# Two rows of x to a partition, and a convolution on quarters of TensorE's array

## The chip, the cores and the metric

The kernel runs on one core of a Trainium2 chip. The time is device microseconds (us) of that core. Before the change the median of three runs is 176.09 us (176.07 to 176.24). TensorE (PE in the profile) multiplies into PSUM; VectorE (DVE) and ScalarE (ACT) copy PSUM out; GpSimd (POOL) issues the loads, SyncE (SP) most stores.

## What is computed

```
x   : 8 x 3264 x 192      weight : 8 heads x 7 taps      w_r, w_i : 64 x 192 x 192     w_ch : 192 x 192
w   = softmax(weight)
c   [b, s, h] = sum over k of w[h, k] * x[b, s - 6 + k, h]        causal, zeros ahead of row 0; 24 channels a head
C   = rfft(c over s), first 64 modes;   Y = C times (w_r + i w_i), mode by mode
y   = irfft(Y, 3264 rows);              u = c + y
out = u + relu(u @ w_ch)
```

Everything is multiplied in bf16 and summed in fp32; the result is fp32.

## The kernel before, in words

**Load.** x is cut into four pairs of sequences (q = 0 to 3). Each sequence is cut in halves of 1632 rows, and a half into 6 blocks (b) of 256 rows and a rest of 96 rows. The loads are issued by GpSimd, which also casts fp32 to bf16 on the way. `load_unit` (L169) loads 128 rows of the four half sequences of a pair at a time: partition p holds row p, so each packet is one row of 192 values, 384 B in bf16. `load_rest` (L179) loads the rests in 4 DMAs of 112 partitions. All of x stays in SBUF in `xall`. Behind x in the same queue come `moe_w_ch` and then the mode weights W (`load_w`, L299): 16 groups g of two DMAs each. Groups 0 to 7 go into `ct` of q = 2 and 3, groups 8 to 11 into a ring of four buffers in `arena`, groups 12 to 15 into the same ring again once the product of the group four before has been made (L501).

**First stage.** `units` (L53 to 55) lists the pieces in order, from q = 0 up and within a q from the last block down: for q = 0 five small ones, then three per q with two blocks each, the last one with the rest. For each unit (loop at L454) `conv_pass` (L312) runs four times, for two heads at a time. The convolution is a product with a banded matrix `bd3` of 128 rows: a main product and one for the six rows from the tile before. Each takes all 128 rows of the array and one half (64) of its columns; its outputs come in two row parities (`a`), so that afterwards partition p holds rows 2p and 2p + 1. The result is copied from PSUM (three pairs of banks, `cz`, in rotation) back into `xall`, three passes by ScalarE (L346), one by VectorE (L344). `fold` (L348, VectorE) makes the sum and the difference of the two halves of each sequence in `cpm`; `dft` (L354) multiplies them with the cosine and sine table `ftab` into the 64 modes (even modes need sums, odd ones differences, so sums and differences go to the two column halves). After the last unit of a q, `xtrans` (L372) turns its modes into the layout of the W products (`xt`). `c_bank` (L420) transposes the convolved rows into `ct`, eight transposes to a PSUM bank and then one copy (L393 to 398, VectorE three times in five, else ScalarE); `g_bank` (L400) does the same for the table of the inverse transform. These 42 transpose banks (`tjobs`, L435) are a list from which the code takes some wherever TensorE is to have work: one per unit from the seventh unit on (L465), ten between the last unit and the first W product (L474 to 488).

**Second part of the load.** The loop at L827 runs over the 16 groups of W. `mix(g)` (L493) is the product with group g, which waits for its W. Beside it run transpose banks in the number that the tuple in L827 gives, `mix_copy` and `mix_trans` for odd g, from g = 8 to 12 the products of five pairs of second-stage items ahead of time (`c_beside`, L662, in two phases), and a filler (`keep_busy`, L815). Banks and `c_beside` share four PSUM banks (`lt`).

**Second stage.** After g = 15, for each of 104 items (128 partitions, one row parity, two sequences) five products per row half of the array make c @ w_ch plus the inverse transform (`product`, L635), ScalarE clamps (L690), VectorE adds and SyncE stores (L712, L732). A planner written in the kernel (`second_stage`, L743) sets their order. The two row halves of the array take turns on a PSUM bank by a `nop` that waits for the other half's last product (L639).

The order on each engine is the order of the program (`manual_schedule`, L150).

Of the kernel before, what the change touches and what calls it, by code (L numbers as in the profile page):

```python
# [19 lines left out]
def kernel(  # L20
# [19 lines left out]
    P = 128  # L40
# [8 lines left out]
    PW = 32 + KK - 1  # L49
# [3 lines left out]
    UNITS0 = ((5, 1, 0), (4, 1, 0), (3, 1, 0), (1, 2, 0), (0, 1, 1))  # L53
    UNITS = ((4, 2, 0), (2, 2, 0), (0, 2, 1))
    units = [(q,) + u for q in range(NQ) for u in (UNITS if q else UNITS0)]

# [12 lines left out]
    xall = sb("xall", [NQ, 2, TQ, D], BF16)  # L69
    band = sb("band", [max(H * 2 * P, MODES // 8 * 2 * D)], BF16)  # L70
# [8 lines left out]
    wb = sb("wb", [D], BF16)  # L79
    ident = sb("ident", [P], BF16)  # L80
    ascale = sb("ascale", [1], F32)
    halfpi = sb("halfpi", [1], F32)
    sgn = sb("sgn", [1], F32)
    NK = 5
# [7 lines left out]
    yall = band[:, :].rearrange("p (n g d) -> p n g d", g=2, d=D)  # L92
    dram = ctx.enter_context(tc.tile_pool(name="dram", bufs=1, space=bass.MemoryType.DRAM))
    yrows = dram.tile([2, MODES // 2, 2 * B, D], BF16, tag="yrows", name="yrows")
    bd3 = band[:, 0:H * 2 * P].rearrange("p (h c) -> p h c", h=H)
# [18 lines left out]
    xdone = xall[:, 0, :, :, :].rearrange("p t k d -> p (t k d)")  # L114
# [18 lines left out]
    packed = temp(G4 * PW, BF16)  # L133
# [9 lines left out]
    masks = temp(KK * PW, U16)  # L143
# [3 lines left out]
    cpm = arena[:, NWA * WGB - FB:NWA * WGB].rearrange("p (r a k d) -> p r a k d", r=2, a=2, k=4)  # L147
    assert pos[0] <= NWA * WGB - FB
# [20 lines left out]
    def load_unit(q, b0, nb, rest):  # L169
        for t in range(2 * b0, 2 * b0 + 2 * nb):  # L170
            k = 2 + 4 * (t // 2)
            src = bass.AP(tensor=x.tensor, offset=x.offset + (2 * q * S + P * t) * D,
                          ap=[[D, P], [HS * D, 4], [1, D]])
            nc.gpsimd.dma_start(out=xall[:, q, t % 2, k:k + 4, :], in_=src)  # L174


    R0 = P - RR - 16

    def load_rest():  # L179
        for i in range(2):  # L180
            for t in range(2):
                off = (i * S + HS * (2 - t) - (P - R0)) * D
                src = bass.AP(tensor=x.tensor, offset=x.offset + off,
                              ap=[[D, P - R0], [2 * S * D, NQ], [1, D]])
                nc.gpsimd.dma_start(out=xall[R0:P, :, t, i, :], in_=src)

# [4 lines left out]
    load_unit(*units[0])  # L191
# [5 lines left out]
    for u in units[1:4]:  # L197
        load_unit(*u)
    load_rest()
    nc.vector.memset(packed, 0.0)  # L200
    nc.scalar.copy(out=bd3[:, :, PW:2 * P], in_=packed[:, 0:1].unsqueeze(2).to_broadcast([P, H, 2 * P - PW]))
# [6 lines left out]
    for k in range(KK):  # L208
        nc.vector.tensor_scalar(out=masks[:, PW * k:PW * (k + 1)], in0=cidx, scalar1=qoff[:, 0:1],
                                scalar2=float(KK - 1 - k), op0=ALU.add, op1=ALU.is_equal)  # L210
# [20 lines left out]
    pk3 = packed.rearrange("p (h c) -> p h c", h=G4)  # L231
    for k in range(KK):
        nc.vector.copy_predicated(out=pk3,
                                  mask=masks[:, PW * k:PW * (k + 1)].unsqueeze(1).to_broadcast([P, G4, PW]),
                                  data=ta3[:, :, k:k + 1].to_broadcast([P, G4, PW]))
    for g in range(4):
        for r in range(4):
            dst = bd3[32 * r:32 * r + 32, G4 * g:G4 * (g + 1), 32 * r:32 * r + PW]
            srcv = pk3[32 * g:32 * g + 32, :, :]
# [9 lines left out]
    def table(step):  # L249
# [10 lines left out]
        else:  # L260
            nc.vector.memset(xall[0:R0, :, :, 0:2, :].rearrange("p q t i d -> p (q t) (i d)"), 0.0)
# [3 lines left out]

    for u in units[4:6]:
        load_unit(*u)
# [4 lines left out]

    nc.gpsimd.memset(ident[:], 0.0)
    select(ident[:], 1.0, 0, [[-1, P]])

    nc.gpsimd.memset(order, 0.0)
    nc.gpsimd.memset(perm, 0.0)
    for c in range(2):
        cols = slice(MODES * c, MODES * (c + 1))
        ov = order[:, cols].rearrange("p (j r) -> p j r", r=2)  # L280
        pv = perm[:, cols].rearrange("p (j r) -> p j r", r=2)
        select(ov, 1.0, -JH * c, [[-1, JH], [-2 * JH, 2]])
        select(pv, 1.0 if c else -1.0, -JH * (1 - c), [[-1, JH], [-2 * JH, 2]])
    for u in units[6:8]:
        load_unit(*u)
    for u in units[8:]:
        load_unit(*u)
# [24 lines left out]
    def conv_pass(q, b0, nb, rest, h2):  # L312
        z = next_pair()
        nk = 4 * nb + 2 * rest
        k0 = 2 + 4 * b0 - 2 * rest

        def put(j, a, half, main, k, n, t, ks, step=1):
            h = 2 * h2 + j
            c0 = a + (0 if main else P)
            o = z[64 * half:64 * half + 64, j, GRP * nk * a:GRP * nk * (a + 1)].rearrange(  # L320
                "p (k e) -> p k e", e=GRP)[:, k - k0:k - k0 + step * (n - 1) + 1:step, :]
            nc.tensor.matmul(o, bd3[:, h, c0:c0 + P - 1:2],  # L322
                             xall[:, q, t, ks:ks + n, GRP * h:GRP * h + GRP],
                             start=(main and a == 0), stop=not main, tile_position=(0, 64 * half),
                             skip_group_check=True)

        for j in range(2):
            for a in range(2):
                for half in range(2):
                    put(j, a, half, True, k0, nk, half, k0)  # L330
# [562 lines left out]
```

## Time and profile before

| | |
|---|---|
| median of three runs | 176.09 us |
| the profiled execution | 175.52 us |
| its span on the core | 173.7 us |
| busy: PE, DVE, ACT, POOL | 149.5, 125.6, 118.8, 66.0 us |
| last DFT of the last unit but one ends the convolution's stretch (L366) | 68.81 us |
| first product with W (L498) | 77.70 us |
| product g = 14 | 105.10 us |

The span is the time from the first instruction to the last on the core; the profiled execution's time holds 1.8 us more, around it. In the lists, L is a line of the kernel, and an arrow in brackets names what ended the idle time before an instruction. A matmul's duration is modelled and matmuls overlap, so the pace is read from the starts of two rows and the count between them.

### The profile page before, as it was taken

To read this page: it belongs to the slowest core of one execution; us is meant where nothing else is said; L and a number is where in the kernel's file an instruction comes from. 1 tells how busy PE (TensorE), PEld (TensorE's weight loads), DVE (VectorE), ACT (ScalarE), POOL (GpSimd) and SP (SyncE) were. 2 spreads that over 40 slices of the span, in tenths; PEclk is the share of its full clock that TensorE was granted. 3 is DMA by queue.
4 is the path that set the end of the run, shared out by engine and by line. 5 is a ranking of instruction groups with operands and counts; after the bars stand their busy time and mean duration, and the time that the engine had idled before them with its cause. 6 is when DMAs were issued, how large, how long until landed. Compare 5 with 4: busy or idle time off the path is not lost.

```text
span 173.7 us, 6647 instructions
## 1 busy us (share of the span) xinstructions
PE 149.5 (86%) x2837; PEld 127.8 (74%) x2837; DVE 125.6 (72%) x246; ACT 118.8 (68%) x224; POOL 66.0 (38%) x108
## 2 busy tenths in 40 slices
PE   0044898899999999799998899999999999999980
PEld 0043797789889889577865565788999988999950
DVE  3892868476778778675545542499998999999990
ACT  6369356658686686755874654588889899898850
POOL 7977997775775584344234300420000000000000
PEclk9999999999999999999999999999999999999995
DMA  2999999999999999999999996359969999999996
GB/s 17 166 173 189 193 188 191 191 189 192 191 190 191 192 204 206 206 206 206 207 208 206 207 205 115 88 191 389 388 233 396 351 357 383 337 339 385 386 356 196
DMA packets 51650, 40.85 MB, mean 235 GB/s; under 512 B 30020, under 2 KB 51524, under 8 KB 51620
## 3 DMA queue, kind: packets, MB, share of 16 engines
q0 software_dynamic: 36400, 20.06, 83.2%
q1 hardware_dynamic: 14948, 20.16, 32.5%
q8 instruction: 22, 0.36, 0.8%
q10 hardware_dynamic: 272, 0.20, 0.3%
q14 instruction: 8, 0.07, 0.1%
HBM read 39.62 MB, written 20.45 MB: 346 GB/s over the span
## 4 chain that ended last, share of the span: by engine, by line
DMA 46%; PE 37%; POOL 9%; issue 3%; DVE 1%; POOLq 0%; DVEq 0%
DMA xall<-in_x_dram 23%; PE outleft L644 18%; DMA arena<-in_moe_w_i_dram 13%; DMA ct<-in_moe_w_i_dram 11%; PE sumright L644 8%; PE mixright L644 8%; POOL xall L174 7%; DVE xall L712 1%; PE sumright L498 1%; PE trleft L429 1%; POOL loose L270 1%; PE sumright L818 0%; PE mixright L526 0%; PE mixright L548 0%; POOL arena L303 0%
## 5 line engine op out<-in xcount | busy, mean ns | idle before, releaser
L322 PEld LDWEIGHTS <-band 128*64 128x64 bf16 x944 | 38.7, 121 | 18.3 <-ACT band L241 11.1
L644 PEld LDWEIGHTS <-ct 64*128 64x128 bf16 x624 | 41.0, 94 | 4.8 <-PE trleft L644 0.5
L322 PE MATMUL cvleft<-xall,band 128*64 128x192 bf16 (+4 forms) x640 | 30.5, 248 | 13.9 <-ACT band L241 11.1
L644 PE MATMUL outleft<-mixa,gtab 64*128 64x384 bf16 x182 | 41.9, 323 | 0.1
L174 POOL DMA_DIRECT2D xall<-in_x_dram x48 | 36.0, 760 | 10.2 <-DMA xall<-in_x_dram 8.4
L644 PEld LDWEIGHTS <-gtab 64*128 64x128 bf16 x416 | 30.9, 94 | 3.0 <-PE outleft L644 1.1
L644 PE MATMUL outleft<-wa,ct 64*128 64x192 bf16 x208 | 30.4, 243 | 0.0
L351 DVE TENSOR_TENSOR arena<-xall 128x1536 bf16<-128x1536 bf16 (+1 forms) x28 | 22.4, 840 | 8.2 <-ACT xall L346 7.8
L690 ACT ACTIVATE outleft<-outleft 128x384 f32<-128x384 f32 x53 | 24.4, 477 | 4.6 <-PE outleft L644 2.3
L346 ACT CAST xall<-cvleft 128x768 bf16<-128x768 f32 (+3 forms) x29 | 21.4, 756 | 8.8 <-PE cvleft L322 7.3
L644 PE MATMUL sumright<-mixa,gtab 64*128 64x384 bf16 x92 | 25.8, 323 | 0.0
L644 PE MATMUL mixright<-mixa,gtab 64*128 64x384 bf16 x90 | 25.8, 323 | 0.0
L644 PE MATMUL outleft<-wb,ct 64*128 64x192 bf16 x104 | 23.3, 243 | 0.0
L398 DVE COPY ct<-trleft 128x1024 bf16<-128x1024 bf16 (+1 forms) x19 | 12.4, 662 | 12.7 <-PE trleft L429 7.8
L322 PE MATMUL cvright<-xall,band 128*64 128x192 bf16 (+4 forms) x304 | 15.9, 247 | 1.6 <-DVE xall L344 1.2
L396 ACT COPY ct<-trleft 128x1024 bf16<-128x1024 bf16 x13 | 13.2, 1012 | 4.6 <-PE trleft L426 2.4
L712 DVE TENSOR_TENSOR arena<-outleft,xall 128x384 f32<-128x384 f32 x27 | 14.4, 553 | 2.5 <-PE outleft L644 2.1
L346 ACT CAST xall<-cvright 128x768 bf16<-128x768 f32 (+3 forms) x13 | 9.8, 751 | 8.4 <-PE cvright L322 6.1
L644 PE MATMUL sumright<-wa,ct 64*128 64x192 bf16 x88 | 14.2, 243 | 0.0
L644 PE MATMUL mixright<-wa,ct 64*128 64x192 bf16 x80 | 13.8, 243 | 0.0
L426 PEld LDWEIGHTS <-xall 128*128 128x128 bf16 x208 | 11.7, 98 | 2.6 <-issue 0.3
L690 ACT ACTIVATE sumright<-sumright 128x384 f32<-128x384 f32 x26 | 12.3, 477 | 1.4 <-PE sumright L644 0.3
(147 smaller groups left out, 283.2 us busy)
## 6 DMA issues: line engine op xcount, KB each, us to landing
xall<-in_x_dram POOLq DMA_DIRECT2D x48, 192.0 KB, 7.9
out_dram<-arena SPq DMA_DIRECT2D x23, 384.0 KB, 4.0
out_dram<-xall SPq DMA_DIRECT2D x13, 384.0 KB, 4.1
out_dram<-ct SPq DMA_DIRECT2D x8, 384.0 KB, 4.6
ct<-in_moe_w_r_dram POOLq DMA_DIRECT2D x8, 288.0 KB, 9.4
ct<-in_moe_w_i_dram POOLq DMA_DIRECT2D x8, 288.0 KB, 10.4
arena<-in_moe_w_r_dram POOLq DMA_DIRECT2D x8, 288.0 KB, 10.5
arena<-in_moe_w_i_dram POOLq DMA_DIRECT2D x8, 288.0 KB, 10.9
```

Source lines behind the costliest of these rows:

```text
L174: nc.gpsimd.dma_start(out=xall[:, q, t % 2, k:k + 4, :], in_=src)
L270: nc.gpsimd.affine_select(out=dst, in_=dst, compare_op=ALU.not_equal, fill=fill, base=base, pattern=pattern, channel_multiplier=1)
L322: nc.tensor.matmul(o, bd3[:, h, c0:c0 + P - 1:2], xall[:, q, t, ks:ks + n, GRP * h:GRP * h + GRP], start=(main and a == 0), stop=not main, ...
L346: nc.scalar.copy(out=dst, in_=srcv)
L351: nc.vector.tensor_tensor(out=cpm[:, r, :, 0:2 * nb, :], in0=src[:, :, :, 0, :], in1=src[:, :, :, 1, :], op=op)
L396: nc.scalar.copy(out=out, in_=in_)
L398: nc.vector.tensor_copy(out=out, in_=in_)
L426: nc.tensor.transpose(o, cv[:, blk, 0:P], ident[:])
L429: nc.tensor.transpose(o[64 * i:64 * i + 64, :], cv[:, i, P:D], ident[:], tile_position=(0, 64 * i))
L644: m = nc.tensor.matmul((Z[s % NZ] if bank is None else bank)[:, cols], l, r, start=start, stop=stop, skip_group_check=True)
L690: act = nc.scalar.activation(out=z, in_=z, func=ACT.Relu)
L712: add = nc.vector.tensor_tensor(out=o[:, :, a, :], in0=Z[s % NZ][:, 0:2 * D].rearrange("p (i d) -> p i d", i=2), in1=c_rows(q, kk)[:, a, : ...
```

## The change

1. **x comes two rows to a partition.** Partition p of a block gets rows 2p and 2p + 1 in one packet of 768 B (in bf16); a DMA loads 128 partitions of one half and two sequences, still 192 KB, two to a block. The rest takes 4 DMAs of 48 partitions. The 16 partitions ahead of a rest, once zeros, get the last 32 rows of the block before, moved by a product (`rows_ahead`), and copied by both ScalarE and VectorE.
2. **The convolution runs on quarters.** Input parity b to output parity a, 64 rows to 64 columns: four products per (a, b), one on each quarter of the array, the two of the upper row half (`src` 0) at once, the two of the lower row half three steps later (`LAG`). Each output parity has a PSUM bank of its own, and the lower row half starts on a bank only when the upper one has left it (a `nop` with a wait, twice per head). The band holds 258 columns a head in place of 256, and is made from 144 columns in place of 76, with four masks in place of seven.
3. **Six large units**, from q = 3 down to q = 0, that may span two q: 4, 4, 4, 5, 3 and 4 blocks, one head at a time. Six heads are copied by ScalarE and heads 3 and 6 by VectorE (half and half in the first unit). The previous unit's folds are issued after heads 1, 3 and 5, into three buffers that now fill the whole arena; its DFT comes after the last head. No transposes run in the convolution any more.
4. **The last unit has no folds**: its DFT multiplies both halves with `ftab` and with `fneg` (the same, odd modes negated) on the full array, 18 products.
5. **Transposes**: a row of `ct` is cut in three full 128 x 128 blocks in place of two full and two half ones; the second stage gets a third copy of weights (`wc`) for it. Twelve banks stand between the last unit and the first W product, and the tuple beside the W products becomes (1, 2, 2, 2, 2, 2, 2, 3, 3, 3, 3, 3, 2, 2, 0, 0).

```diff
-    UNITS0 = ((5, 1, 0), (4, 1, 0), (3, 1, 0), (1, 2, 0), (0, 1, 1))
-    UNITS = ((4, 2, 0), (2, 2, 0), (0, 2, 1))
+    units = [[(3, 4, 2, 0), (3, 2, 2, 0)], [(3, 0, 2, 1), (2, 4, 2, 0)], [(2, 2, 2, 0), (2, 0, 2, 1)],
+             [(1, 4, 2, 0), (1, 2, 2, 0), (1, 1, 1, 0)], [(1, 0, 1, 1), (0, 4, 2, 0)], [(0, 2, 2, 0), (0, 0, 2, 1)]]
...
+            q, b = blocks.pop(0)
+            for h in range(2):
+                k = 2 + 4 * b + 2 * h
+                src = bass.AP(tensor=x.tensor, offset=x.offset + (2 * q * S + HS * h + 2 * P * b) * D,
+                              ap=[[2 * D, P], [S * D, 2], [1, 2 * D]])
+                nc.gpsimd.dma_start(out=xall[:, q, k:k + 2, :, :].rearrange("p k t d -> p k (t d)"), in_=src)
...
+    def rows_ahead(q):
+        k = 2 + 4 * (NBH - 1)
+        z = next_pair()
+        for i in range(2):
+            for h in range(2):
+                nc.tensor.matmul(z[64 * (1 - h):64 * (1 - h) + 64, i, 0:2 * D], ahead[64:P, :],
+                                 xall[64:P, q, k + 2 * h + i, :, :].rearrange("p t d -> p (t d)"), start=True,
+                                 stop=True, tile_position=(64, 64 * (1 - h)), skip_group_check=True)
+        for h, engine in enumerate((nc.scalar.copy, nc.vector.tensor_copy)):
+            r = slice(64 * (1 - h), 64 * (1 - h) + R0)
+            engine(out=xall[r, q, 0:2, :, :].rearrange("p i t d -> p i (t d)"), in_=z[r, :, 0:2 * D])
...
+    def conv_head(u, h, engine):
+        z = next_pair()
+        f0, f1 = extent(u)
...
+        def put(src, dst, c, a, b, fa, fb, back=0, start=False, stop=False):
+            r = slice(64 * src, 64 * src + 64)
+            base = c + (0 if a == b else PB - 1 + a)
+            return nc.tensor.matmul(z[64 * dst:64 * dst + 64, a, GRP * (fa - f0):GRP * (fb - f0)],
+                                    bd3[r, h, base:base + 64], xflat[r, fa - back:fb - back, b, cols], start=start,
+                                    stop=stop, tile_position=(64 * src, 64 * dst), skip_group_check=True)
+
+        def later(a, b, name):
+            if a == b:
+                nop = nc.tensor.nop()
+                tc.add_manual_dep(nop.ins, name[-1], mybir.DependencyInfo(
+                    mybir.DependencyClass.Sync, mybir.DependencyReason.DATA), reason="row tiles take turns on a bank")
+            put(1, 1, 0, a, b, f0, f1, stop=a != b)
+            for k, (fa, fb) in enumerate(spans):
+                put(1, 0, 64, a, b, fa, fb, 4, stop=a != b and k == len(spans) - 1)
+            if a == 1 and b == 0:
...
+                if engine == "v":
+                    nc.vector.tensor_copy(out=dst, in_=srcv)
+                else:
+                    nc.scalar.copy(out=dst, in_=srcv)
+
+        for a in range(2):
+            last = []
+            for b in (a, 1 - a):
+                put(0, 1, 64, a, b, f0, f1, start=a == b)
+                last.append(put(0, 0, 0, a, b, f0, f1, start=a == b).ins.name)
+                upper.append(lambda a=a, b=b, name=last: later(a, b, name))
+                flush(LAG)
...
+            if cpm is None:
+                ops.append((ftab[:, t, :], call[:, q, 1 + 2 * b, a, :, :], slice(0, P)))
+                ops.append((fneg[:, t, :], call[:, q, 2 + 2 * b, a, :, :], slice(0, P)))
...
     for k, u in enumerate(units):
...
+        for q, b0, nb, rest in u:
+            if b0 + nb == NBH:
+                rows_ahead(q)
+        todo = []
+        for h in range(H):
+            conv_head(u, h, "v" if h in ((1, 3, 5, 7) if k == 0 else (3, 6)) else "a")
+            if k == 0 and h in (1, 3, 5):
+                table(h // 2)
+            if prev and h in (1, 3, 5):
+                piece = prev.pop(0)
+                todo.append((*piece, fold(*piece)))
+        flush()
+        for q in pend:
+            xtrans(q)
+        pend = [d[0] for d in todo if d[3]]
+        for d in todo:
+            dft(*d)
+        prev = list(u)
+    lt += hand_out("left", "tr", (1, 1, 1, 1))
     for g in range(NWC + NWA):
         load_w(g)
-    trans_banks(3)
+    trans_banks(2)
     rot[0] = 2
-    xtrans(NQ - 1)
+    for q in pend:
+        xtrans(q)
+    for piece in prev:
+        dft(*piece, None)
+    trans_banks(8)
+    rot[0] = 2
+    xtrans(0)
     ye = hand_out("right", "mix", (1, 1))
     trans_banks(2)
...
-    for g, beside in enumerate((0, 1, 1, 2, 2, 2, 1, 2, 2, 2, 2, 2, 2, 2, 0, 0)):
+    for g, beside in enumerate((1, 2, 2, 2, 2, 2, 2, 3, 3, 3, 3, 3, 2, 2, 0, 0)):
```

More of the change, by code (lines that the diff above doesn't have):

```diff
@@ L142 @@
     qoff = temp(1, F32)
-    masks = temp(KK * PW, U16)
+    NE4 = (KK + 1) // 2
+    masks = temp(NE4 * PW, U16)
     sidx = temp(NTF, F32)
@@ L817, in keep_busy @@
         for _ in range(n):
-            nc.tensor.matmul(sums[bank][:, 0:2 * D], ident[:], xall[:, 0, 0, 0:2, :], start=True, stop=True,
+            nc.tensor.matmul(sums[bank][:, 0:2 * D], ident[:], call[:, 0, 0, 0, :, :], start=True, stop=True,
                              skip_group_check=True)
@@ L825, in beside_pair @@
             tb[0] += 2 * phase
-    for g, beside in enumerate((0, 1, 1, 2, 2, 2, 1, 2, 2, 2, 2, 2, 2, 2, 0, 0)):
+    for i in range(2):
+        nc.scalar.copy(out=wc[64 * i:64 * i + 64, :], in_=wa[64 * (1 - i):64 * (1 - i) + 64, :])
+    for g, beside in enumerate((1, 2, 2, 2, 2, 2, 2, 3, 3, 3, 3, 3, 2, 2, 0, 0)):
         d = g // 2
```

224 lines of the change are left out of this document (100 added, 124 removed).

## The prediction

> **What bounds the kernel now.** I read the page from the top: the busy shares, then the slices, then the chain.
>
> ```profile
> PE 149.5 (86%) x2837; PEld 127.8 (74%) x2837; DVE 125.6 (72%) x246; ACT 118.8 (68%) x224; POOL 66.0 (38%) x108
> DMA  2999999999999999999999996359969999999996
> GB/s 17 166 173 189 193 188 191 191 189 192 191 190 191 192 204 206 206 206 206 207 208 206 207 205 115 88 191 389 388 233 396 351 357 383 337 339 385 386 356 196
> DMA 46%; PE 37%; POOL 9%; issue 3%; DVE 1%; POOLq 0%; DVEq 0%
> ```
>
> Two halves show. For 24 slices (104 us) the DMA engines are full with loads: x, then the mode weights W at a higher rate. After a dip the results go out, and the chain of waits is TensorE's. So the chain names DMA for the load half. But a full DMA engine only says that there is always something to move; whether TensorE keeps up must be read from its own timeline.
>
> ```profile
> 59.22 0.85 PE L322 MATMUL cvleft<-xall,band 128*64 128x192 bf16 x16
> 59.90 0.82 PE L366 MATMUL sumright<-arena,ftab 128*64 128x384 bf16 x8
> 60.55 0.49 PE L366 MATMUL sumright<-xall,ftab 128*64 128x384 bf16 x4
> ...
> 62.20 0.22 PE L378 MATMUL cvleft<-loose 128*64 128x128 bf16 x1
> ...
> 62.59 0.85 PE L322 MATMUL cvright<-xall,band 128*64 128x192 bf16 x16
> ...
> 68.81 0.86 PE L366 MATMUL sumright<-arena,ftab 128*64 128x384 bf16 x8
> ...
> 77.70 0.71 PE L498 MATMUL sumright<-ct,mixa 128*16 128x192 bf16 x24 [0.17 <-ACT mixa L389]
> ...
> 87.73 0.46 PE L498 MATMUL sumright<-arena,mixa 128*16 128x192 bf16 x12
> ...
> 93.64 0.46 PE L498 MATMUL sumright<-arena,mixa 128*16 128x192 bf16 x12 [0.72 <-DMA arena<-in_moe_w_i_dram]
> ...
> 96.51 0.46 PE L498 MATMUL sumright<-arena,mixa 128*16 128x192 bf16 x12 [0.43 <-DMA arena<-in_moe_w_i_dram]
> 96.90 1.07 PE L426 MATMUL trleft<-ident,xall 128*128 128x128 bf16 x16
> 97.90 0.34 PE L644 MATMUL trleft<-wa,ct 64*128 64x192 bf16 x4
> 98.07 0.25 PE L644 MATMUL trleft<-wb,ct 64*128 64x192 bf16 x2
> 98.25 0.40 PE L526 MATMUL mixright<-ident,band 128*128 128x128 bf16 x4
> 98.48 0.33 PE L818 MATMUL sumright<-xall,ident 128*128 128x384 bf16 x1
> 98.74 0.34 PE L644 MATMUL trleft<-wa,ct 64*128 64x192 bf16 x4
> ...
> 105.10 0.46 PE L498 MATMUL sumright<-arena,mixa 128*16 128x192 bf16 x12
> ```
>
> The convolution ends at 68.8, the products with W start at 77.70 (groups g = 0 and 1), g = 8 is at 87.73, g = 10 at 93.64, g = 14 at 105.10. Only from g = 10 on does TensorE wait for W, and only 0.72, 0.43 us and less per group of 2.87 us. **TensorE is thus nearly as late as the DMA.** A faster load alone gains little unless TensorE's own path to g = 14 gets shorter; that path is what I add up. From g = 14 on nothing in the order of work changes, so the end moves as g = 14 moves.
>
> **What TensorE's pieces cost (same rows).** Sixteen convolution products of 192 columns take 59.22 to 59.90: 42 ns each, where two column halves run side by side. At 2.4 columns per ns (the 16 transposes of 128 columns, 96.90 to 97.90, say about the same) 192 columns in two halves would be 40 ns. A DFT pair takes 0.163 us (eight products, 59.90 to 60.55). xtrans is 0.4 us (62.20 to 62.59). A transpose bank (8 transposes) is 0.50 us. In the W loop a group costs 0.40 for mix, 0.35 for each phase of c_beside, 0.23 for mix_trans (every other group), 0.27 for keep_busy. Test on the old loop: from g = 0 to g = 8 it has 8 mixes, 11 banks and 4 mix_trans, 3.2 + 5.5 + 0.9 = 9.6; the rows say 10.03, so I add 4%.
>
> **The load (part 1 of the change).**
>
> ```profile
> 0.00:10.00 10.00, 0.00 (x0) 0.00 (x0) 6.43 (x31) 4.63 (x5) 8.86 (x18) 1.00 0.93 100
> 10.00:57.00 47.00, 40.91 (x883) 36.99 (x885) 32.81 (x55) 31.09 (x50) 34.91 (x54) 1.00 1.59 190
> 62.00:102.00 40.00, 37.24 (x757) 28.82 (x751) 24.22 (x41) 26.13 (x40) 16.67 (x28) 1.00 1.21 206
> ...
> xall<-in_x_dram POOLq DMA_DIRECT2D x48, 192.0 KB, 7.9
> xall<-in_x_dram POOLq DMA_DIRECT2D x4, 168.0 KB, 7.8
> 35.05 1.18 PE L322 MATMUL cvleft<-xall,band 128*64 128x192 bf16 x24 [0.66 <-DMA xall<-in_x_dram]
> ```
>
> The first three rows are stages of the windows view and end in granted clock, DMA share and GB/s; two are DMA issues, the last is TensorE's timeline. x moves at 190 in packets of 384 B (192 bf16), W at 206 in packets of 1152 B. Per engine (a sixteenth) that is 32.3 and 89.5 ns a packet; a straight line through both gives 3.7 ns plus 74.5 ns per 1000 B, so the new 768 B packets take 60.9 ns: 202 GB/s. The bounds are 190 (no gain) and 206; I take 202 as the line between the two rows. x shrinks from 48 x 192 KB + 4 x 168 KB = 10.13 MB to 10.03 (the rest has 48 partitions of 768 B in place of 112 of 384). With 1.0 MB moved by 10 us, x ends at 58.05 before and 54.7 after: **3.35 us earlier**, and W with it. POOL still issues 48 + 4 DMAs, half the packets each, in the same gaps between its memsets and selects; it is 38% busy and waits on landings, so I cost it at nothing.
>
> The Trainium skill (DMA: Bandwidth & Descriptors, section Specifications) says that below 512 B a transfer falls short of line rate, as the engine must read before it writes. By that rule the new packets run at W's 206, which takes 0.6 us off the sum below; the rows show the slower 384 B, none shows 768 B.
>
> When is data usable? At 35.05 TensorE gets the 24th x DMA, 5.41 MB with the rest, while 5.76 had moved: landing lags by 1.8 us. Each unit needs its own blocks (0.393 MB each), the rest from the second on, and the block below. So unit 1 (9 blocks) can start at 27.3, unit 3 (18) at 44.8, unit 4 (21) at 50.7, unit 5 (all) at 56.5.
>
> **The convolution (part 2).** A unit is 8 heads of 4 steps; a step is 4 products on the four quarters of the array, N = 24 x (16, 18, 18, 20, 14, 18) columns, and 3 steps of lag are half empty at the unit's end: 35 steps. If four quarters run side by side a step takes N/2.4, but not below 4 x 42 = 168 ns. That gives 6.3, 6.3, 7.0, 5.9, 6.3 us for units 1 to 5. No row shows quarters. Bounds: four at a time as above, or only two, twice the time. I take four, since the row at 59.22 shows column halves side by side and the second stage row halves (the stage row's PE column holds the count):
>
> ```profile
> 115.00:167.00 52.00, 52.00 (x893) 48.28 (x891) 49.04 (x97) 45.69 (x105) 0.00 (x0) 1.00 0.98 355
> ```
>
> 893 products of on average 269 columns (three of 192, two of 384) in 52 us are 58 ns each; one alone would need 112. The two waits per head before the lower rows take a bank stand behind two more steps of the upper rows (0.34 us), so I cost them at nothing; uncovered they cost up to 0.1 us each, 1.6 per unit.
>
> **Evacuation and folds.** Elements copied out of PSUM are the same.
>
> ```profile
> L351 DVE TENSOR_TENSOR arena<-xall 128x1536 bf16<-128x1536 bf16 x20 | 18.3, 954 | 7.4 <-ACT xall L346 7.4
> L344 DVE CAST xall<-cvleft 128x768 bf16<-128x768 f32 x4 | 3.8, 957 | 2.2 <-PE cvleft L322 1.7 <-DMA xall<-in_x_dram 0.5
> L344 DVE CAST xall<-cvleft 128x960 bf16<-128x960 f32 x2 | 2.3, 1157 | 0.1
> L346 ACT CAST xall<-cvleft 128x768 bf16<-128x768 f32 x15 | 11.7, 802 | 4.8 <-PE cvleft L322 3.3 <-DMA xall<-in_x_dram 1.5
> L398 DVE COPY ct<-trleft 128x1024 bf16<-128x1024 bf16 x15 | 10.2, 690 | 9.5 <-PE trleft L429 5.0 <-PE trleft L426 4.4
> L396 ACT COPY ct<-trleft 128x1024 bf16<-128x1024 bf16 x13 | 13.2, 1012 | 4.6 <-PE trleft L426 2.4 <-PE trleft L429 1.8
> ```
>
> ScalarE's six copies of a unit fit (6 x 0.8 to 0.96). VectorE has a queue problem in unit 4: first the rows_ahead copy (0.96), then two folds of unit 3 (two instructions of 0.954 each), and only behind them the copy of head 3 (0.86). Head 6 takes head 3's banks and must wait.
>
> **The path of TensorE, us.** Unit 1 from 27.3: 33.6, DFT of unit 0 (8 pairs, 1.3): 34.9. Unit 2: 41.2, DFT 1.63: 42.8. Unit 3 waits for data, 44.8: 51.8, xtrans and DFT: 53.8. Unit 4: rows_ahead 0.35, 54.2, and 0.2 more until its products have drained; VectorE is done with copy, folds and head 3 at 54.4 + 0.96 + 3.82 + 0.86 = 60.0, head 6 starts at 60.2 in place of 54.2 + 24 x 0.168 = 58.2 (**2.0 lost**), 11 steps: 62.1, xtrans and DFT: 64.1. Unit 5: 70.4, DFT 1.3: 71.7. Then 12 banks (6.0), two xtrans (0.8), and the DFT without sums: 18 products of 384 columns on the full width, 0.16 each, 2.9. That form costs 1.3 more than paired ones and saves 3.8 us of folds that would have stood alone here. **The products with W start at 81.4**, against 77.70.
>
> And more is left by then. The old order has 18 of its 42 transpose banks behind it at this point (8 of them inside the convolution), the new one 12. g = 0 to 8: 3.2 + 16 banks 8.0 + 0.9 = 12.1, with 4% 12.6: 94.0. g = 8 to 12: 0.40 + 3 banks 1.5 + 0.35 + 0.27 + 0.35 = 2.87 each, 0.5 for two mix_trans: 12.0. g = 12: 0.40 + 1.0 + 0.97 = 2.37; g = 13: 0.40 + 0.23 + 3 keep_busy 0.81 = 1.44. **g = 14 at 109.8, 4.7 us after 105.10.** W is there in time: W 11 lands at 96.51 - 3.35, about 93, its ring of four refills from g = 8 at 94 on, and W 12 is wanted at 106; the DMA engines fall idle in between. The copies keep up on average (3 banks: 1.8 x 0.69 and 1.2 x 1.01 in 2.87 us).
>
> **Sum.** 175.52 + 4.7 = 180.2 for a profiled execution (span 173.7). The median of the runs is 176.09, 0.57 more; so I predict **180.8**. Set-up of the band changes (144 columns for 76, 4 masks for 7), but what it adds lies before unit 1's 27.3. wc and fneg are under 1 us on engines with slack. The second stage has the same products.
>
> The change also opens a gap: unit 0 (5 blocks usable at 16.6, then 5.9 of steps) ends near 22.5 and unit 1 starts at 27.3.
>
> ```profile
> 169.00:170.00 1.00, 0.00 (x0) 0.00 (x0) 0.47 (x1) 0.00 (x0) 0.00 (x0) 1.00 1.11 384
> 170.00:171.00 1.00, 0.00 (x0) 0.00 (x0) 0.00 (x0) 0.00 (x0) 0.00 (x0) 0.52 0.96 298
> ```
>
> After TensorE's last work (before 169) the granted clock falls from 1.00 to 0.52 within two us, so unit 1 may start at half clock. The Trainium skill (TensorE: Matmul & The Clock Gate, Part 1) gives about 3.4 us of work to get it back, by my estimate 1.7 us lost. The 2.0 us that TensorE has before unit 3's data take it up; were they gone, it would be paid in full: 182.5.
>
> **Rivals.** (1) TensorE is quicker than I think and W sets the end. From the start of the W products to g = 14 there are 28.4 us of work, so below a start at 76.7 the kernel is faster, and from 73.3 down W is the bound at -3.35: **172.7**. For it: the load does end earlier. Against: even with no VectorE wait (2.0) and no wait for unit 3's data (2.0) the start is 77.4. Chance 0.14, most of it part of the way. (2) The quarters run only two at a time: 31.8 us more from unit 1 on, less 4.0 of waits: **209**. Against it the two rows named; 0.05. (3) Three banks beside c_beside make five users of four banks per group; copies then stall TensorE by up to one copy's 0.69 in each of five groups (3.5), and the bank turns cost their 1.6 in units 3 to 5 (4.8): **184 to 189**; 0.13. (4) x stays at 190: unit 3 starts 2.1 later: 182.9; this lies in the forecast's range.
>
> **How the numbers follow.** Forecast with its spread (177.5 to 184): 0.61. Rival 3: 0.13, rival 2: 0.05, a small loss (176.5 to 177.5): 0.04, within 0.2%, about what a measurement here can tell from none: 0.03, faster: 0.14. So faster 0.14, same 0.03, slower 0.83; the range 175.5 to 186.5 leaves out the far ends of rivals 1, 2 and 3.
>
> **What would show it.** Right: x at 200 GB/s or more in the stage row; a gap before unit 1; convolution steps of 170 to 200 ns; head 6 of unit 4 waiting for VectorE; the first W product near 81; g = 14 near 110 with no wait for DMA, and DMA slices below 9 after 90 us. Wrong: W products before 77, or waits for W at g = 10 to 14 as now.

## The result, and the profile after

The kernel after the change takes 184.30 us (median of four runs, 184.18 to 185.44), the kernel before, run beside it, 176.08 (175.97 to 176.24): a ratio of 1.0481 with a 95% interval of 1.0438 to 1.0523. It is **8.2 us slower**; the forecast was 180.8, its range 175.5 to 186.5. The profiled execution is the slowest of the four (185.44 us, span 183.7).

The page of the kernel after: busy time, the slices, and the chain of waits by engine.

```profile
PE 158.6 (86%) x2635; PEld 120.3 (65%) x2635; DVE 126.2 (69%) x244; ACT 121.3 (66%) x222; POOL 67.1 (37%) x108
DMA  3999999999999999999900998249988999999995
GB/s 20 192 199 200 201 202 201 163 191 201 202 201 202 206 207 207 206 206 205 173 6 6 173 198 144 45 110 362 362 273 303 380 360 367 351 357 383 367 367 170
PE 65%; DVE 10%; DMA 8%; POOL 6%; ACT 5%; issue 3%; POOLq 0%; ACTq 0%; DVEq 0%
```

From the third slice on x moves at 199 to 202 GB/s in all slices but two, 190 before. Then the DMA engines stand still for two slices (92 to 101 us): W's ring is full, and no product has freed a buffer. In the chain DMA falls from 46% to 8%: the load is no longer what ends last.

TensorE's timeline of the kernel after: start, duration, what it does, and in brackets the idle time before it and what ended it.

```profile
36.17 1.71 PE L384 MATMUL cvleft<-xall,band 64*64 64x432 bf16 x26
...
38.20 0.41 PE L384 MATMUL cvright<-xall,band 64*64 64x432 bf16 x4
38.72 0.37 PE L384 MATMUL cvleft<-xall,band 64*64 64x432 bf16 x2
...
41.46 0.37 PE L384 MATMUL cvleft<-xall,band 64*64 64x432 bf16 x2
...
43.64 0.84 PE L442 MATMUL sumright<-arena,ftab 128*64 128x384 bf16 x8
...
47.76 0.39 PE L384 MATMUL cvright<-xall,band 64*64 64x480 bf16 x2 [0.51 <-DVE xall L348]
...
59.23 0.33 PE L384 MATMUL cvleft<-xall,band 64*64 64x336 bf16 x2 [0.90 <-DVE xall L348]
...
63.46 0.86 PE L384 MATMUL cvleft<-xall,band 64*64 64x336 bf16 x19 [1.27 <-DVE xall L400]
...
67.36 0.98 PE L384 MATMUL cvleft<-xall,band 64*64 64x432 bf16 x10
...
74.83 0.52 PE L442 MATMUL sumright<-arena,ftab 128*64 128x384 bf16 x4
...
85.93 0.47 PE L566 MATMUL sumright<-ct,mixa 128*16 128x192 bf16 x12 [0.28 <-ACT mixa L465]
...
114.78 0.46 PE L566 MATMUL sumright<-arena,mixa 128*16 128x192 bf16 x12
```

L384 is a product of the convolution, L442 the DFT, L566 the product with W. The first product with W is at 85.93 (77.70 before, 81.4 in the forecast), g = 14 at 114.78 (105.10 before, 109.8 in the forecast), and none of these rows waits for a DMA. The convolution's units last longer than their steps. Unit 2 is the plain case: 36.17 to 43.64 is 7.47 us, where 35 steps of 0.18 are 6.3. At 38.20 four products, one step, take 0.52 us in place of 0.18, with no wait named. Unit 5 (67.36 to 74.83) takes 7.47 as well.

Stages of the windows view of the kernel after (the last three columns are granted clock, DMA share, GB/s):

```profile
10.00:54.00 44.00, 36.65 (x584) 23.16 (x584) 28.56 (x52) 27.16 (x38) 35.95 (x53) 0.96 1.29 196
...
26.00:27.00 1.00, 0.54 (x12) 0.34 (x13) 0.62 (x1) 0.35 (x1) 0.72 (x1) 0.89 1.32 201
27.00:28.00 1.00, 1.00 (x22) 1.00 (x18) 1.00 (x2) 0.05 (x1) 1.00 (x3) 0.50 1.32 202
...
30.00:30.50 0.50, 0.50 (x17) 0.39 (x13) 0.50 (x1) 0.27 (x1) 0.50 (x1) 0.80 1.31 201
```

Over the load's stretch the mean rate is 196 GB/s, because of a dip at 33 to 38 us (163 in the slice there); no product waits for x behind it, and in e5 the same stretch reads 201. In this execution the granted clock halves soon after the start of unit 1: the mean of 0.89 puts the fall near 26.8, that of 0.80 the rise near 30.2.

Two copies from ScalarE's and VectorE's timelines of the kernel after:

```profile
45.94 0.79 ACT L348 CAST xall<-cvright 16x768 bf16<-16x768 f32 x1 [0.61 <-PE cvright L343]
46.76 0.95 DVE L348 CAST xall<-cvright 16x768 bf16<-16x768 f32 x1 [2.68 <-ACT xall L348]
```

They are the copies of `rows_ahead` (16 partitions, but 0.79 and 0.95 us) at the start of unit 3: VectorE's begins only when ScalarE's is done. Both must be done before the pair of banks is free; at 47.76 a head waits for it.

### The profile page after: what moved, and what is told of

Its sections match the earlier page's. It is cut to its first block, busy times and chain, and to the rows that moved or that the text cites. A ratio compares the mean times of both kernels' runs of the same rounds, so it can differ in the third digit from the quotient of the medians.

```text
span 183.7 us, 6228 instructions
## 1 busy us (share of the span) xinstructions
PE 158.6 (86%) x2635; PEld 120.3 (65%) x2635; DVE 126.2 (69%) x244; ACT 121.3 (66%) x222; POOL 67.1 (37%) x108
## 3 DMA queue, kind: packets, MB, share of 16 engines
q0 software_dynamic: 23088, 19.96, 68.8%
## 4 chain that ended last, share of the span: by engine, by line
PE 65%; DVE 10%; DMA 8%; POOL 6%; ACT 5%; issue 3%; POOLq 0%; ACTq 0%; DVEq 0%
PE outleft L713 17%; PE trleft L500 9%; DMA xall<-in_x_dram 8%; PE sumright L713 8%; PE mixright L713 7%; PE cvleft L384 7%; PE sumright L442 6%; POOL xall L193 5%; DVE arena L420 4%; PE cvright L384 3%; DVE xall L400 3%; PE sumright L566 3%; PE trleft L713 2%; PE mixright L594 2%; ACT xall L402 1%
## 5 line engine op out<-in xcount | busy, mean ns | idle before, releaser
L384 PE MATMUL cvleft<-xall,band 64*64 64x432 bf16 (+6 forms) x552 | 43.8, 349 | 10.8 <-DMA xall<-in_x_dram 6.2
L384 PEld LDWEIGHTS <-band 64*64 64x64 bf16 x832 | 30.0, 113 | 28.4 <-issue 9.4
L384 PE MATMUL cvright<-xall,band 64*64 64x432 bf16 (+5 forms) x280 | 27.8, 346 | 0.5 <-DVE xall L348 0.5
L402 ACT CAST xall<-cvleft 128x864 bf16<-128x864 f32 (+3 forms) x20 | 17.1, 858 | 15.4 <-PE cvleft L384 9.0
L713 PE MATMUL outleft<-wa,ct 64*128 64x192 bf16 x104 | 22.9, 243 | 0.0
L713 PE MATMUL outleft<-wc,ct 64*128 64x192 bf16 x104 | 21.7, 243 | 0.0
L500 PE MATMUL trleft<-ident,xall 128*128 128x128 bf16 x312 | 20.0, 220 | 0.0
L400 DVE CAST xall<-cvleft 128x864 bf16<-128x864 f32 (+3 forms) x12 | 12.3, 1021 | 11.2 <-PE cvleft L384 6.6
L500 PEld LDWEIGHTS <-xall 128*128 128x128 bf16 x312 | 17.5, 98 | 2.2 <-ACT loose L446 0.3
L402 ACT CAST xall<-cvright 128x864 bf16<-128x864 f32 (+3 forms) x14 | 11.9, 851 | 6.9 <-PE cvright L384 6.5
```

What stands on the lines that cost most here:

```text
L384: return nc.tensor.matmul(z[64 * dst:64 * dst + 64, a, GRP * (fa - f0):GRP * (fb - f0)], bd3[r, h, base:base + 64], xflat[r, fa - back:fb ...
L500: nc.tensor.transpose(o, cv.rearrange("p i d -> p (i d)")[:, P * blk:P * blk + P], ident[:])
L713: m = nc.tensor.matmul((Z[s % NZ] if bank is None else bank)[:, cols], l, r, start=start, stop=stop, skip_group_check=True)
```

## The experiments

**The theory** after the first reading: units 2 to 5 wait for ScalarE and VectorE to copy the pairs of banks out. **The rivals**: TensorE itself loses the time, in the turns of row halves on a bank; or unit 1's start at half clock does. Ratios are to the kernel before on the same chip; 0.01 is 1.76 us. The kernel after stands at 1.0481.

**e1: the lower row half one step behind.** `LAG = 3` becomes `LAG = 1`.

> The changed kernel with the lower row half one step behind the upper in place of three. Theory A (evacuation: a head holds its pair of PSUM banks for 4 steps and the lag, and with three pairs TensorE waits for the copies): each head gives its pair back two steps (0.36 us) earlier and each unit's tail is two steps shorter, so units 1 to 5 lose about 1 us each, 178 to 181 us in place of 184.3. Theory B (the turns of the row halves on a bank are what costs on quarters): the wait for the upper half's last product loses its cover, 0.1 to 0.27 us sixteen times a unit, 189 us or more.

209.8 us (median; 200.2 to 212.5, too spread for an interval). TensorE's timeline of e1: the starts of two heads in unit 1, a DFT, and two rows of unit 5 that are one head apart:

```profile
30.83 1.58 PE L384 MATMUL cvleft<-xall,band 64*64 64x432 bf16 x12
...
32.89 1.58 PE L384 MATMUL cvright<-xall,band 64*64 64x432 bf16 x12
...
47.12 2.77 PE L442 MATMUL sumright<-arena,ftab 128*64 128x384 bf16 x16
...
92.42 1.45 PE L384 MATMUL cvright<-xall,band 64*64 64x432 bf16 x12
...
93.71 2.73 PE L384 MATMUL cvleft<-xall,band 64*64 64x432 bf16 x28
```

A head takes 2.06 us in unit 1 and 1.29 in unit 5, in place of 0.72. Two things are mixed here. Up to about 58 us this execution works at half pace: the DFT's 16 products take 2.77 us, and 1.49 in the changed kernel. (The trace holds no record of the clock before 58.6 us, and a stretch without a record is printed as 1.00.) In unit 5 the pace is the full one, and there the two turns of a bank per head add 1.29 less 0.72: about 0.29 us each when no other step lies between. At half pace, where four steps are 1.44, they come to 0.31 each. That holding a pair shorter helps is refuted in this form; sixteen such turns (4.6 us a unit) cost more than it saves. How much of the 25 us is half pace, and why it lasted so long, was not tested.

**e2: VectorE copies heads 0 and 7 in place of 3 and 6.**

```diff
-            conv_head(u, h, "v" if h in ((1, 3, 5, 7) if k == 0 else (3, 6)) else "a")
+            conv_head(u, h, "v" if h in ((1, 3, 5, 7) if k == 0 else (0, 7)) else "a")
```

> The changed kernel with heads 0 and 7 copied by VectorE in units 1 to 5 in place of heads 3 and 6. Theory A: head 3's copy no longer stands behind the folds in VectorE's queue; the waits before head 6 go (0.8 in unit 3, 1.3 in unit 4, some 0.9 in units 2 and 5): 181 to 182.5 us. Theory B (the products on quarters themselves are slow): 184.3, unchanged.

Ratio 1.0386 (1.0353 to 1.0419): 1.7 us faster than the changed kernel. The waits for head 3's copy, 0.78 us in unit 3 and 1.27 in unit 4, are gone.

**e3: the next unit's `rows_ahead` ahead of xtrans and DFT** in place of behind them.

> The changed kernel with rows_ahead of the next unit ahead of xtrans and the DFT in place of behind them. Theory A: its two copies (0.8 on ScalarE, then 0.95 on VectorE, one after the other) lie beside the DFT, the waits of 0.5 us (unit 3) and 0.9 us (unit 4) for them go and the folds start about 2 us earlier: 181 to 182.5 us. Theory B: 184.3, unchanged.

Ratio 1.0397 (1.0362 to 1.0432): 1.5 us faster. No wait for L348 is left; its copies now lie beside the DFT. The folds behind them come earlier too, so that the wait for head 3's copy in unit 4 shrinks from 1.27 to 0.42 us.

**e4: filler products before unit 1**, six behind head 5 and ten after the last head of unit 0.

> The changed kernel with 6 products of 384 columns on the full array into an unused bank after head 5 of unit 0 and 10 after its end, where TensorE waits. If the half clock at the start of unit 1 (26.7 to 29.0 us at 0.52) costs time that nothing makes up later: 1.1 us less, 183.2. If later waits take it up, as the prediction had it: 184.3.

Ratio 1.0618 (1.0581 to 1.0656), slower by 2.4 us. The fillers stand ahead of unit 1's `rows_ahead`, in TensorE's timeline of e4:

```profile
25.98 0.35 PE L343 MATMUL cvleft<-xall,ahead 64*64 64x384 bf16 x2
...
28.35 0.37 PE L384 MATMUL cvleft<-xall,band 64*64 64x432 bf16 x2 [0.64 <-DVE xall L348]
...
32.79 0.98 PE L384 MATMUL cvleft<-xall,band 64*64 64x432 bf16 x20 [0.95 <-DVE xall L400]
34.98 1.33 PE L442 MATMUL sumright<-arena,ftab 128*64 128x384 bf16 x14
```

Its copies and the folds behind them come later, and unit 1 now waits 0.64 and 0.95 us for VectorE. Its DFT starts at 34.98, no earlier than in the profiled execution of the changed kernel (34.75), whose unit 1 did begin at half clock.

**e5: e2 and e3 together.**

> Copies 0 and 7 by VectorE, and the rows ahead early, together. Theory A, two causes that add: head 3's copy behind the folds costs 1.6 us, the rows-ahead pair and copies cost 1.5 us, both gone gives 3.1 us less than the changed kernel, about 181.0. Theory B, one slack shared by both (what one edit frees, the next wait takes): no more than the better of the two, 182.4. Neither theory gets below the kernel before.

181.24 us, ratio 1.0297 (1.0265 to 1.0330): 3.2 us faster than the changed kernel. That is the sum of the two, but each of these differences is known to about 0.9 us only. The traces say that the two overlap in part: at full clock the first product with W is at 84.61 without either edit (e12, below), at 83.20 in e2, 82.72 in e3 and 82.10 here. Both causes lie in VectorE's queue.

**e6: the last unit with folds again** (undoes part 4), `dft(*piece, None)` becomes `dft(*piece, fold(*piece))`.

> The last unit with sums and differences again, the half products on two column halves in place of 18 products on the full width. Theory A, as in the prediction: 3.8 us of folds (4 instructions of 0.95 us) stand alone ahead of the DFT, which itself gets 1.3 us shorter: 2.5 us slower, about 186.8. Theory B: the two transpose banks and the xtrans ahead of it (1.4 us) hide a fold and a half: 1.1 us slower, 185.4.

201.1 us. This says nothing on folds: their memory is the ring in which W 8 to 11 had been asked for by then, so the folds wait for these loads and overwrite them.

**e10: the same, with the folds ahead of the loads of W.**

> The last unit with sums and differences again, the folds ahead of the loads of W into the same memory. Against the changed kernel (184.3 by its ratio). Theory A, as in the prediction: 3.8 us of folds stand alone less 1.3 us of shorter DFT: 2.5 us slower, 186.8. Theory B: two transpose banks and an xtrans hide 1.4 us of them: 1.1 us slower, 185.4. Theory C: the copies of the transposes queue behind the folds on VectorE and nothing is hidden, the xtrans too: 3.5 us or more slower, 187.8.

200.5 us, ratio 1.1434 (1.1398 to 1.1471). The DFT still came behind those loads in the order of the program, so it found W where the folds were, and waited for it. A row of TensorE's timeline of e10:

```profile
83.38 1.17 PE L442 MATMUL sumright<-arena,ftab 128*64 128x384 bf16 x5 [6.87 <-DMA arena<-in_moe_w_i_dram]
```

**e12: folds, DFT, and only then the loads of W 8 to 11.**

```diff
+    halves = [fold(*piece) for piece in prev]
-    for g in range(NWC + NWA):
+    for g in range(NWC):
         load_w(g)
...
-        dft(*piece, None)
+        dft(*piece, halves.pop(0))
+    for g in range(NWC, NWC + NWA):
+        load_w(g)
```

> The last unit with sums and differences again, and the loads of W groups 8 to 11, which take the memory of the folds, issued only behind the DFT that reads them (in e6 and e10 that DFT came behind these loads in the order of the program, and waited for them). Against the changed kernel (184.3 by its ratio). Theory A, as in the prediction: 3.8 us of folds stand alone less 1.3 us of shorter DFT: 2.5 us slower, 186.8. Theory B, from the rows of e10: the folds (3.56 us) start with the two transpose banks and end 1.7 us after xtrans, so from the first of these banks to the end of the DFT it is 3.2 + 1.0 = 4.2 us in place of 4.4: no difference, 184.0 to 184.6. Theory C: W 8 to 11, issued 3 us later, come too late for g = 8: a wait for DMA there and 1 us or more slower.

184.41 us, ratio 1.0500 (1.0474 to 1.0526): no difference that this can tell from the changed kernel. TensorE's and VectorE's timelines of e12:

```profile
74.65 3.56 DVE L420 TENSOR_TENSOR arena<-xall 128x1536 bf16<-128x1536 bf16 x4 [0.58 <-ACT xall L402]
75.05 1.07 PE L500 MATMUL trleft<-ident,xall 128*128 128x128 bf16 x16
76.42 1.30 PE L442 MATMUL sumright<-arena,ftab 128*64 128x384 bf16 x9
78.27 0.81 PE L442 MATMUL sumright<-arena,ftab 128*64 128x384 bf16 x7 [0.55 <-DVE arena L420]
...
79.33 3.63 PE L500 MATMUL trleft<-ident,xall 128*128 128x128 bf16 x62
```

The folds run from 74.65 to 78.21, beside two transpose banks, xtrans and the first piece's DFT. From the first bank (75.05) to the next ones (79.33) it is 4.28 us; in the changed kernel 76.26 to 80.66, 4.40.

**e7: the new loads alone**, in the kernel before: the 48 loads of blocks, not the four of the rests. Each partition then holds other rows than the old convolution assumes, so that only the time counts.

```diff
-            src = bass.AP(tensor=x.tensor, offset=x.offset + (2 * q * S + P * t) * D,
-                          ap=[[D, P], [HS * D, 4], [1, D]])
+            src = bass.AP(tensor=x.tensor, offset=x.offset + (2 * q * S + HS * (t % 2) + 2 * P * (t // 2)) * D,
+                          ap=[[2 * D, P], [S * D, 2], [1, 2 * D]])
...
```

> The kernel before, with only its 52 loads of x changed: the 48 loads of 192 KB move packets of 768 B. Each partition then holds other rows of x than the convolution assumes, so the numbers that come out are not those of the reference; every instruction but the loads is the old one. Theory A, TensorE is nearly as late as the DMA: x ends some 2 to 3 us earlier, but only the waits for W at g = 10 to 14 go (0.72 + 0.43 us and three below 0.4): 1.5 to 2 us faster, 173.5 to 174.0. Theory B, the load is the bound, as the chain of waits names it: the whole gain of x, 3.0 us: 172.5. Theory C, the landing of x was never waited for and W's groups neither: same, 175.5.

172.83 us, ratio 0.9828 (0.9787 to 0.9869): **3.0 us faster** than before, 2.3 to 3.8 by the interval. A stage of the windows view and TensorE's timeline of e7:

```profile
30.00:54.00 24.00, 23.90 (x508) 21.52 (x509) 17.81 (x22) 17.45 (x23) 17.22 (x25) 1.00 1.31 202
...
76.21 0.71 PE L498 MATMUL sumright<-ct,mixa 128*16 128x192 bf16 x24 [0.17 <-ACT mixa L389]
...
101.53 0.46 PE L498 MATMUL sumright<-arena,mixa 128*16 128x192 bf16 x12
```

The first product with W comes 1.49 us earlier, g = 14 3.57 us. The convolution before the change follows x (its waits for x, one of which the prediction quoted, are gone), and so do the waits for W. The load thus was the bound, more than the forecast held; and the rest of the change costs not 8.2 but some 11.5 us (1.0481 less 0.9828).

**e8: the lower row half four steps behind**, `LAG = 4`.

> The lower row half follows four steps behind in place of three. Theory A, a pair's holding time sets the pace of units 2 to 5: a head holds its pair a step longer, 0.18 us per rotation of three heads, 0.06 us per head, 40 heads: 2.4 us slower, about 186.4. Theory B, the stretches of 0.2 to 0.4 us that no wait is named for are turns of the banks that three steps don't quite cover: one step more covers them, 2 to 4 us faster, 180 to 182.

Ratio 1.0569 (1.0536 to 1.0601): 1.5 us slower than the changed kernel. TensorE's timeline of e8, unit 2:

```profile
37.11 0.35 PE L384 MATMUL cvright<-xall,band 64*64 64x432 bf16 x2
37.79 0.37 PE L384 MATMUL cvleft<-xall,band 64*64 64x432 bf16 x2 [0.33 <-ACT xall L402]
...
39.71 0.37 PE L384 MATMUL cvright<-xall,band 64*64 64x432 bf16 x2 [0.23 <-ACT xall L402]
...
40.74 0.47 PE L384 MATMUL cvright<-xall,band 64*64 64x432 bf16 x3
```

The gaps that had no name now have one: the copy of the head three before. Head 3 starts at 37.79 and head 6, on the same banks, at 40.74, 2.95 us later; in the changed kernel 38.72 and 41.46, 2.74 us. The difference is about a step. That the turns of the banks make these gaps is refuted, since one step more would have covered them.

In the changed kernel's unit 2 the copies account for the gaps. ScalarE's and VectorE's timelines:

```profile
37.79 1.66 ACT L402 CAST xall<-cvleft 128x864 bf16<-128x864 f32 x2 [2.04 <-DMA xall<-in_x_dram]
...
40.35 1.06 DVE L400 CAST xall<-cvleft 128x864 bf16<-128x864 f32 x1 [1.00 <-ACT xall L402]
```

Head 0 starts at 36.17 and holds its pair for seven steps, 1.26 us; its copy of 0.88 us starts at 37.79 and ends at 38.67, and head 3 starts on this pair at 38.72. Head 3's own copy ends at 41.41, and head 6 starts at 41.46.

**e9: e5 with the DFT inside the unit**: that of the first two pieces after heads 4 and 6.

> The kernel of e5 (181.24), with the DFT of the previous unit's first two pieces issued after heads 4 and 6 of the unit in place of after its last head. Theory A, the products wait for PSUM pairs that ScalarE and VectorE have not copied out yet, although no wait is named at most of these places: the DFT needs no pair and fills these waits, of which units 2 to 5 hold some 4 us (7.6 + 8.1 + 6.4 + 7.6 us against 6.3 + 7.0 + 5.9 + 6.3): 3 to 4 us faster, 177.2 to 178.2. Theory B, the loss lies in TensorE itself (turns of a bank, a slower pace of quarters): the same products in another order, 180.7 to 181.5.

183.04 us, ratio 1.0431 (1.0407 to 1.0454): 2.4 us *slower* than e5, which neither theory expected. VectorE's and TensorE's timelines of e9 at the start of unit 4:

```profile
54.67 1.16 DVE L400 CAST xall<-cvleft 128x960 bf16<-128x960 f32 x1 [3.78 <-PE cvleft L384]
55.75 0.95 DVE L348 CAST xall<-cvright 16x768 bf16<-16x768 f32 x1
...
55.88 0.86 PE L384 MATMUL cvleft<-xall,band 64*64 64x336 bf16 x11 [0.52 <-DVE xall L400]
```

The DFT between the units had been the time in which the last head's copy and the rows ahead were moved; without it, unit 4 begins with a wait for them. And a DFT in front of a head's last steps should hold back its copy by just as long (read from the order of the program), so that the next heads wait as before: unit 2 with its DFT and rows ahead takes 9.67 us in e9 and 9.71 in e5. That waiting for copies sets the pace is not refuted by this, but that TensorE's work can be put into these waits is, in this form.

**e11: e9 with eight transpose banks in the gap before unit 1.**

> The kernel of e9, with eight transpose banks in the gap between units 0 and 1: the two of the inverse table and six of the four blocks that unit 0 has convolved. For this the transposes and the second stage begin with the sequences that the convolution has first. Six banks less stand between unit 5 and the first product with W. Theory A, TensorE's path from unit 1 to g = 14 is the bound and the gap is free: 6 x 0.5 = 3 us off e9, 1 us more where unit 1 started at half clock; by theory A of e9 that is 174, by its theory B 177.5. Theory B: the eight banks with their copies (5 x 0.69 on VectorE, 3 x 1.01 on ScalarE) hold up unit 1 by 1 to 2 us: 1 to 2 us off e9. Theory C: W comes to be the bound; the product g = 14 cannot then be earlier than in e7 (101.5), and the time not below e7's 172.8.

191.21 us, ratio 1.0853 (1.0810 to 1.0895): 7.4 us slower than e9. TensorE's timeline and a stage of the windows of e11:

```profile
24.55 0.62 PE L478 MATMUL cvleft<-ident,ftab 128*128 128x128 bf16 x8 [0.29 <-DVE xall L400]
26.00 0.50 PE L478 MATMUL cvleft<-ident,ftab 128*128 128x128 bf16 x6 [0.84 <-DVE gtab L474]
...
34.32 0.53 PE L343 MATMUL cvleft<-xall,ahead 64*64 64x384 bf16 x2
...
27.00:34.30 7.30, 4.65 (x40) 4.14 (x39) 2.96 (x5) 2.05 (x3) 6.15 (x9) 0.54 1.31 201
```

The second bank of a pair waits for the copy of the first (0.84 at 26.00), so eight banks take 24.55 to 34.32, 9.8 us in place of 4. In the last 7.3 us of it TensorE is busy for 64%, and the granted clock is 0.54. Unit 1's rows ahead come at 34.32, in e9 at 25.18. The gap was in fact short: unit 0 ended near 24.3.

## Why the prediction was right, and where its terms were off

The direction and its mechanism were right: TensorE is late, and the load's gain is spent behind it. The time lies 3.5 us above the forecast. Of the signs that the prediction names, the steps of 0.18 us, head 6's wait in unit 4, no wait for W and the idle DMA engines came; the stage row reads 196 GB/s and not 200, the gap before unit 1 is short (24.3 to 25.0), and the first W product is 4.5 us late.

| step of the prediction | forecast | measured |
|---|---|---|
| rate of x | 202 GB/s | 199 to 202 in most slices, 196 on the mean |
| a step of four quarters, N = 432 | 0.18 us | 0.18 us |
| end of unit 1 | 33.6 us | 34.75; 33.59 in e3, whose clock does not fall |
| unit 2 | 6.3 us | 7.47 |
| unit 3 | 7.0 after a data wait of 2.0 | 9.3, no data wait |
| unit 4, rows ahead and a wait included | 8.3 | 8.5 |
| unit 5 | 6.3 | 7.47 |
| from unit 5's DFT to the first W product | 9.7 after a DFT of 1.3 | 9.67 after 1.43 |
| first W product to g = 14 | 28.4 | 28.85 |

**The mis-sized term is units 2 to 5**, units 2 and 5 above all, with 1.17 us each. They were costed as TensorE's steps, and the copies were compared with them only as sums per engine ("ScalarE's six copies of a unit fit"). But a head holds its pair of banks for 7 of the 12 steps that three pairs give, and the copy (0.88 or 1.06 us) and its signals come behind; e8 shows that a further step of holding is paid. The Trainium skill (TensorEngine Tiling (Array Packing), PSUM Bottleneck) says that tiling speeds up TensorE but not the evacuation of PSUM; this case agrees: the step is at its 0.18 us, three heads take 2.74 us in place of twelve such steps, 2.16. Two more waits stand in VectorE's queue. For unit 4 the prediction saw the copy of head 3 behind the folds (2.0 us; the row at 63.46 says 1.27), but not that the rows ahead take a pair of their own, whose two copies run one after the other and hold up an early head (0.51 at 47.76, 0.90 at 59.23). e2 and e3 price the two causes at 1.7 and 1.5 us, e5 both together at 3.2, each to about 0.9. That unit 4 came out near its 8.3 is luck: its forecast wait was 0.7 us too long, and one of 0.90 that it did not have came on top. So it is with unit 3, whose waits for copies took the place of the wait for data. And e5 at 181.24 meets the forecast in the sum only; its unit 2 still takes 7.47 us (34.59 to 42.06).

**"A faster load alone gains little" failed.** e7 gains 3.0 us. The step compared W's waits alone; it left out that the old convolution waits for x too. It did not hurt the sum, because the new convolution no longer keeps up with x.

**The bank turns at nothing** were right at three steps of lag: e8 gains nothing from a fourth. The uncovered price of 0.1 us stood on no row and was too low: e1 shows about 0.29.

**The last unit without folds** was credited with 2.5 us. e12 shows no difference: the two banks, xtrans and the first DFT hide the folds, except 0.55 us. The 9.7 us came out right because the form that was costed is the one that ran.

**The clock.** The fall that the prediction held possible came in the profiled execution, and was paid, as unit 3's wait for data that was to take it up did not come: its DFT of unit 0 starts at 34.75, while e3's and e5's profiles, whose clock reads 1.00 there, have it at 33.59 and 33.17. The other three executions of the changed kernel, whose mean clock over the span is 0.988 to 0.994 in place of 0.982, take 1.1 to 1.3 us less, so that the median holds little of it. The clock is back after 3.4 us (26.8 to 30.2); the Trainium skill (TensorE: Matmul & The Clock Gate, Part 1) gives about 3.4 us of work for that, and this trace agrees. e1 does not: its half pace lasts to 58.6 us, although its TensorE is shown busy for 9.18 of the 10 us from 35 on. Why the clock falls in one execution and not in another stays open; e4 shows that fillers on TensorE's queue are no remedy here.

**The rivals.** Rival 3's five users of four banks did not come: the W products' loop takes 28.85 us against 28.4. Rival 2 and rival 4 are refuted by the step of 0.18 us and the 196 to 202 GB/s. The rate of 206, which the prediction gave as the other bound, did not come either. Rival 1 lacked its condition: even e5 starts the W products at 82.10, and 76.7 was wanted.

No version tried is faster than the kernel before and computes the same: e5, the best, is 3.0% slower. Whether copying each bank of a pair by itself, in a tile of its own, shortens the holding was not tried.

## What to carry to other kernels

Where heads rotate through a few PSUM buffers, cost one full turn: the steps for which a buffer is held, plus its copy and signals, against the steps that the rotation gives. Engine sums can fit while every turn waits, and such waits of 0.2 to 0.4 us need not have a name in the profile; the pace between starts shows them. A copy of 16 partitions costs as much as one of 128 (0.79 and 0.95 us here for `rows_ahead`, 0.80 and 0.96 for a head of unit 0 with the same 768 elements), and work between two stages may be what hides the first stage's evacuation, so moving it is not free.

## What the hardware showed that was not expected

Two row halves that take turns on a bank cost about 0.29 us a turn when nothing lies between (e1, unit 5), and nothing that shows with two more steps of 0.18 between (the changed kernel).

Unit 0's steps took 0.32 us, and from 20 us on the same steps took 0.16. The granted clock is printed as 1.00 for both. But the first record of the clock in this trace is at 19.96 us, and a stretch without one is printed as 1.00. 0.32 us for 384 columns is the pace of the recorded half clock, 0.36 for 432 (steps at 27.32, 27.68 and 28.04). TensorE's timeline of the kernel after:

```profile
14.93 0.83 PE L384 MATMUL cvleft<-xall,band 64*64 64x384 bf16 x2
15.25 0.53 PE L384 MATMUL cvright<-xall,band 64*64 64x384 bf16 x2
...
22.90 0.35 PE L384 MATMUL cvright<-xall,band 64*64 64x384 bf16 x2
...
23.07 0.35 PE L384 MATMUL cvright<-xall,band 64*64 64x384 bf16 x2
```

The half pace cost some 2.3 us, and a wait for VectorE at 22.26 another 1.27; that is why unit 0 ended near 24.3 and not at 22.5. All traces of this case begin without a record, up to 13.8 to 23.3 us, and e1 up to 58.6: a printed 1.00 there says nothing.

GpSimd is slow beside VectorE's folds. Its selects (which set up small tables between the loads) take 0.45 to 0.50 us, but the one that fell beside unit 1's folds took 3.36, and no load was issued meanwhile. GpSimd's and VectorE's timelines of the kernel after:

```profile
24.67 0.46 POOL L293 TENSOR_SCALAR_AFFINE_SELECT loose<-loose 128x64 bf16<-128x64 bf16 x1
...
27.73 3.36 POOL L293 TENSOR_SCALAR_AFFINE_SELECT loose<-loose 128x64 bf16<-128x64 bf16 x1
27.25 3.54 DVE L420 TENSOR_TENSOR arena<-xall 128x1536 bf16<-128x1536 bf16 x4
```

In e3, e4, e6, e8, e10 and e12, where it also meets the folds, it takes 3.05 to 4.29 us; in e1, e2, e5 and e9, where it does not, 0.45. The prediction had costed GpSimd at nothing. The dip in x's rate comes a few us later, in e4 too; in e3 the rate stays at 200 in spite of the long select, so that this is its cause is not shown.
